# The order list of an adaLN block on one core, solved anew, with two more products of zeros

## The chip, the cores and the metric

The kernel runs on one core of one Trainium2 chip. The metric is device time in microseconds (us) for one execution. Three runs of the kernel before took 416.54, 415.92 and 416.29 us, median 416.29. The engines named below are TensorE (PE; its weight loads are PEld), VectorE (DVE), ScalarE (ACT), GpSimd (POOL) and SyncE (SP), which here only issues DMAs.

## The reference

An adaLN-conditioned block on 2048 tokens of width 576, all in bf16 at the borders:

```
mod = silu(c) @ w_mod                       # six rows of 576: sa, ca, ga, sb, cb, gb
h = layernorm(x) * (1 + ca) + sa
q, k, v = split(h @ wqkv)                   # 32 heads of 18
phi(t) = [softmax(t @ w_phi), softmax(-(t @ w_phi))]     # 36 features a head
kv = phi(k)^T v ; z = sum(phi(k)) ; o = phi(q) kv / (phi(q) z + 1e-6)
x = x + ga * (o @ wo)
h = layernorm(x) * (1 + cb) + sb
x = x + gb * (relu(h @ w1) @ w2)            # hidden width 4608
```

## The kernel before

The tokens stand in 16 tiles of 128. Everything up to the sum `kv` must have seen all tokens; after it, the feed-forward part runs on eight pairs of tiles (`block(n)`, unchanged by the edit), almost without a pause on PE.

To save products, the kernel folds `w_phi` into the key and query weights and the scale `1 + ca` into all three projections. That is the head of the program. For the keys (weights cut into five row chunks of 128, the last of 64):

- `LK.i` loads the key weights: `LK.1` holds chunks 2 and 3, `LK.2` chunk 4, `LK.0` chunks 0 and 1. `WT.c` (`fold_T`, L329) turns chunk c on PE with six transposes into a PSUM tile, and `WTE.c` copies the result out.
- `F1.c` (`fold`, L339) multiplies the turned chunk by the block-diagonal of `w_phi` (built by `WBD` on DVE). Its PSUM tile is copied out in two parts, `FA1.c` (432 columns) and `FB1.c` (144 columns).
- `SIL` computes silu(c); `MC1.0` and `MC1.1` (`first_mods`, L307) make the shift and the scale as columns, each with 25 products of one column. `MSH` and `MSC` copy them out on DVE.
- `B1`, `Bv` and `B0` (`fold_bias`, L360) make the bias rows of keys, values and queries from the shift; `BE...` copy them out. `SC1.c`, `SCv.c`, `SC0.c` scale the chunks of the three weights.
- For x: `LP` and `LP4` load tiles, `LS.t` are the layernorm sums on DVE, `RS.u` the two activations for the factor, `LX.u` the normalisation. `PT.u` (L256) turns the first two pairs on PE, `PX.u.i` copies them out; the later tiles are turned by DMA (`LT.t`, issued by SP).
- `F0`, `FA0`, `FB0` do for the queries what `F1`, `FA1`, `FB1` do for the keys; their turned weights come by DMA (`LQ.c`).

Then come the projections `K.t`, `V.t`, `Q.t` (`project`, L438), each ten products, with copies `KE`, `VE`, `QE`; the softmax steps of the keys (`MN`, `MX`, `LO`, `HI`, `EX`, `SU`, `SA`, `RC`, `SC`) and queries (the same with a q); the rows of the second modulation (`LM`, `RW`, `RWE`, `RC2`, `RD`); the sum `KVa`, `KVb`, `KVc` (L616) with its copies `KVE`; the first pair's attention (`NU` to `WOE`); and the first feed-forward pair (`G`, `FW`, `RL`, `Y`, with the weights `LW` and `W2`).

The order of all this work is written out as a list of names in the string `order`; no scheduler touches SP, PE, DVE and ACT. Each engine runs its own instructions strictly in the list's order. A name's digits are its arguments. For copies and scalings a last argument picks the engine: for most `.1` is ACT and none is DVE; for `KE`, `VE` and `QE` none is ACT and `.1` is DVE. Where a step waits for another engine, everything behind it on its own engine waits too.

PSUM tiles of the products come from `mm_tile`, three buffers in turn: a step that opens a tile waits until the tile opened three steps before has been copied out. The modulations and the products of zeros use `aux_tile`, two buffers in turn.

A product of zeros is the step `Z.k`, whose number has no meaning: one product of 512 columns that nobody reads. One more runs before the list begins.

```
    def fill(n):
        ps = aux_tile("ps_warm")
        for _ in range(n):
            T_.matmul(ps[:], lhsT=zeros[:, 0:P], rhs=zeros[:], start=True, stop=True)
```

The places where the list is run:

```
    for step in order.split():
        name, *at = step.split(".")
        steps[name](*map(int, at))
```

Of the kernel before, what the change touches and what calls it, by code (L numbers as in the profile page):

```python
# [44 lines left out]
def kernel(  # L45
# [23 lines left out]
    V, A_, G, T_ = nc.vector, nc.scalar, nc.gpsimd, nc.tensor  # L69
# [841 lines left out]
    }  # L911

    order = """
    LH LK.1 WT.3 LP.1 WTE.3.1 WT.2 LS.2 WTE.2.1 LK.2 WT.4 WTE.4.1 WBD LK.0 WT.1 LS.3 F1.2 LP.0 WTE.1 F1.3 FB1.2
    LS.1 SIL F1.1 FA1.2.1 RS.1 LX.1 FA1.3.1 LS.0 WT.0 FA1.1.1 FB1.3.1 F1.4 LA.0 FB1.1.1 WTE.0.1 LA.1 Z.2 PT.1
    PX.1.1 FA1.4.1 F1.0 FB1.0 FB1.4 FA1.0.1 MC1.0 LV MSH LP4.2 PX.1.0 RS.0 LX.0 MC1.1 B1 LQ.2 MSC SC1.4 SC1.0
    SC1.2 LQ.3 BE1.0.1 BE1.1.1 SC1.3 LQ.0 PT.0 Bv LP4.4 SCv.0 PX.0.1 SCv.1 SC1.1.1 LS.4 SCv.2 PX.0.0.1 BEv.0.1
    OPEN CR K.2 LS.6 LS.5 BEv.1.1 SCv.3.1 SCv.4.1 K.1 LQ.4 PM.0 KE.2 LQ.1 KE.1 LS.7 V.3 VE.3 RS.2 K.0 LX.2 V.0
    V.1 KE.0 VE.0 RS.3 LQ.5 F0.4 F0.3 LT.4 VE.1 FA0.4.1 LP4.6 F0.2 FB0.4.1 PM.2 LT.5 FB0.3.1 FA0.2.1 V.2 LS.8
    FA0.3.1 LS.10 LS.11 LS.9 FB0.2.1 RS.4 LX.3 VE.2 F0.1 FB0.1 LX.4 FA0.1.1 LS.14 LT.7 RS.5 LT.9 LT.6 K.3 KE.3  # L920
    F0.0 FA0.0.1 K.4 PM.1 KE.4 FB0.0 K.5 SC0.4.1 KE.5 LS.13 LX.5 LT.11 LS.15 V.4 LS.12 RS.6 VE.4 MN.0 SC0.2 K.7
    KE.7 K.9 SC0.1.1 KE.9 LT.10 SC0.0.1 LT.8 MX.0 LO.0 V.9 VE.9 RS.7 K.6 KE.6 SC0.3 B0 BE0.0.1 BE0.1 K.11 Q.2
    LO.1 LX.6 LM.1 LM.0 LM.2 KE.11 Q.3 QE.2 HI.0 Q.1 Q.0 LX.7 EX.0 MX.1 HI.1 MN.1 QE.3 QE.1 QE.0 K.10 KE.10 SU.0
    SA.0 EX.1 LO.2 RW.1 RWE.1.1 RW.0 HI.2 EX.2 LT.13 LT.15 RWE.0 K.8 qMX.0 PM.3 KE.8 qMN.0 SU.1 K.15 KE.15 V.5
    RC.0 VE.5 V.11 VE.11 LO.3 HI.3 LT.12 MX.2 WOL LT.14 V.14 RC2.0 K.12 EX.3 VE.14 SC.0 RC2.2 Q.7 qHI.0 QE.7
    qLO.0 SA.1 SD.6 SD.7 KE.12 RC.1 qEX.0 K.13 KE.13 SU.2 K.14 KE.14 V.12 MN.2 LO.5 LO.4 SA.2 HI.5 VE.12 W1
    LW.0.0 MX.3 LW.2.0 qEX.1 Q.4 RC.3 QE.4 HI.4 MN.3 RC.2 LW.2.1 RC2.1 LW.1.1 RD.2 V.8 VE.8 V.15 qSU.0 V.7 Q.14
    LO.6 EX.5 qSA.0 VE.15 VE.7 EX.4 SC.3 Q.13 SC.1 Q.8 SU.4 SA.4 HI.6 QE.14 SC.2 LW.1.0 QE.13 QE.8 LO.7 HI.7
    qRC.0 SU.5 SA.5 RC.4 Q.10 V.6 QE.10.1 qSC.0 SC.4 EX.6 VE.6 V.10 SU.6 SA.6 EX.7 V.13 SU.7 VE.10 RC.5 RD.0
    VE.13 SC.5 RC.6 SA.7 SC.6 RC.7 SC.7 qT.0 KVa MCE2 KVb KVc WS.0 Q.12 KVE.1 KVE.0.1 NU.1 Q.9 LW.0.1 QE.12 WS.1  # L930
    NU.0 NUE.1 OT.1 OTE.1 QE.9 Q.6 QE.6 NUE.0 OT.0 OTE.0 WO.1 WO.0 WOE.1 S2.1 Q.11 WOE.0 S2.0 QE.11 R2 X2 Q.15
    Q.5 QE.5 P2 W2.0.0 W2.0.1 LW.3.0 QE.15 W2.2.0 PN PNE G.0 W2.1.0 qMX.1 qMN.2 RL.0 qMN.1 FW.2 qLO.1 qHI.1 RL.2
    FW.1 RL.1 RD.1 qEX.3 LW.3.1 W2.1.1 W2.2.1 qEX.2 G.1 RL.3 qSD.3 FW.4 qSD.2 RL.4 qRC.1 qSC.1 FW.5 qMX.2 qHI.2
    qT.1 RL.5 G.2 RL.6 FW.7 FW.8 NV.0 qLO.2 qEX.4 qSD.4 Y.0.0.0 RL.8 Y.0.0.1 qEX.5 RL.7 NVE.0 OU.0 NV.1 Y.1.0.0
    Y.1.0.1 NVE.1 qSD.5 OU.1 WP.0 WPE.0 Y.1.1.0 S3.0 WP.1 WPE.1 S3.1 R3 qRC.2 Y.0.0.2 Y.1.1.1 Y.1.0.2 X3 XT
    YE.0.0 qSC.2 qT.2 Y.0.1.0 MD.0 YE.1.0 Y.0.1.1 MD.4 MD.3 MD.2 MD.1 Y.0.1.2 Y.1.1.2 YE.1.1 YE.0.1
    """
    for step in order.split():
        name, *at = step.split(".")
# [101 lines left out]
```

## Time and profile before

| | us |
|---|---|
| median of three runs | 416.29 (415.92 to 416.54) |
| the profiled execution | 416.63 |
| its span, first to last instruction | 414.5 |
| PE busy in the span | 406.0 (98%) |
| PE, weight loads | 331.2 (80%) |
| DVE busy | 237.4 (57%) |
| ACT busy | 174.2 (42%) |

The busy times are sums over stages of different kinds. A row of a timeline begins with the start and the length of a group in us; then come the engine, the line of the kernel, the operation with its tiles, shapes and count, and in brackets how long the engine had been idle before, and what ended it. A row of the waits gives the total, the times and the longest wait. A row of a table by stretches gives for each engine its busy time and, in brackets, its instructions.

### The profile page before, as it was taken

To read this page: it belongs to the slowest core of one execution; us is meant where nothing else is said; L and a number is where in the kernel's file an instruction comes from. 1 tells how busy PE (TensorE), PEld (TensorE's weight loads), DVE (VectorE), ACT (ScalarE), POOL (GpSimd) and SP (SyncE) were. 2 spreads that over 40 slices of the span, in tenths; PEclk is the share of its full clock that TensorE was granted. 3 is DMA by queue.
4 is the path that set the end of the run, shared out by engine and by line. 5 is a ranking of instruction groups with operands and counts; after the bars stand their busy time and mean duration, and the time that the engine had idled before them with its cause. 6 is when DMAs were issued, how large, how long until landed. Compare 5 with 4: busy or idle time off the path is not lost.

```text
span 414.5 us, 9208 instructions
## 1 busy us (share of the span) xinstructions
PE 406.0 (98%) x3953; PEld 331.2 (80%) x3953; DVE 237.4 (57%) x612; ACT 174.2 (42%) x279; POOL 11.8 (3%) x39
## 2 busy tenths in 40 slices
PE   6999999999999999999999999999999999999997
PEld 5777777787888788788878887888888888878876
DVE  7879999996776665547345552846192533230011
ACT  5687889945671064016302630452055014302400
POOL 8100010000000000000000000000000000000000
PEclk9999999999999999999999999999999999999999
DMA  8956967079931820502051014204210502010001
GB/s 250 251 118 156 237 157 217 1 144 369 321 72 32 118 47 2 115 16 33 15 102 32 17 33 84 47 2 69 61 35 2 117 18 31 16 32 16 0 2 30
DMA packets 72161, 35.43 MB, mean 85 GB/s; under 512 B 56689, under 2 KB 69754, under 8 KB 72122
## 3 DMA queue, kind: packets, MB, share of 16 engines
q1 hardware_dynamic: 71520, 34.83, 35.9%
q8 instruction: 31, 0.51, 0.5%
q10 hardware_dynamic: 602, 0.02, 0.1%
q14 instruction: 8, 0.07, 0.0%
HBM read 19.27 MB, written 2.37 MB: 52 GB/s over the span
## 4 chain that ended last, share of the span: by engine, by line
PE 87%; DVE 7%; DMA 2%; ACT 2%; issue 1%; SPq 1%; DVEq 0%; ACTq 0%
PE ps_y L849 34%; PE ps_h L806 31%; PE ps_h L798 4%; PE ps_v L438 3%; PE ps_wo L714 3%; PE ps_k L438 3%; PE ps_q L438 2%; DMA x_sb<-in_A_x_dram 2%; PE ps_sum L504 2%; PE ps_wo L438 2%; DVE bst L223 2%; DVE phik L528 1%; PE ps_num L657 1%; PE ps_bias L360 1%; DVE xn L232 1%
## 5 line engine op out<-in xcount | busy, mean ns | idle before, releaser
L811 ACT ACTIVATE H<-ps_h 128x1024 bf16<-128x1024 f32 x72 | 73.7, 1023 | 171.1 <-PE ps_h L798 122.5
L849 PE MATMUL ps_y<-w_sb,H 128*128 128x288 bf16 (+2 forms) x1188 | 143.0, 282 | 0.0
L849 PEld LDWEIGHTS <-H 128*128 128x128 bf16 x1188 | 113.7, 98 | 27.3
L806 PE MATMUL ps_h<-hT,w1a 128*128 128x256 bf16 x640 | 74.9, 273 | 0.3 <-DVE hT L408 0.3
L806 PEld LDWEIGHTS <-w1a 128*128 128x128 bf16 x640 | 61.2, 98 | 9.9 <-issue 2.7
L857 DVE TENSOR_TENSOR outt<-ps_y,row_gb 128x288 bf16<-128x288 f32 (+2 forms) x33 | 14.8, 448 | 85.6 <-PE ps_y L849 85.6
L806 PE MATMUL ps_h<-hT,w1b 128*128 128x256 bf16 x512 | 58.9, 273 | 0.0
L438 PEld LDWEIGHTS <-hT 128*128 128x128 bf16 x480 | 46.4, 98 | 13.4 <-issue 1.2
L806 PEld LDWEIGHTS <-w1b 128*128 128x128 bf16 x512 | 49.9, 98 | 6.5 <-issue 0.6
L719 DVE TENSOR_TENSOR x_sb<-x_sb,ps_wo 128x288 bf16<-128x288 bf16 x28 | 12.7, 454 | 32.8 <-PE ps_wo L714 24.8
L223 DVE BATCH_NORM_STATS2 bst<-x_sb 128x6 f32<-128x288 bf16 x64 | 25.8, 444 | 2.1 <-DMA x_sb<-in_A_x_dram 2.0
L232 DVE TENSOR_SCALAR xn<-x_sb,mv,rstd 128x576 bf16<-128x576 bf16 x32 | 12.2, 424 | 22.1 <-ACT rstd L228 22.1
L438 PE MATMUL ps_k<-wfold,hT 128*128 128x270 bf16 (+1 forms) x160 | 22.1, 288 | 0.3 <-ACT pq L89 0.3
L438 PE MATMUL ps_v<-wv_sb,hT 128*128 128x288 bf16 x160 | 21.4, 286 | 0.2 <-ACT room L89 0.2
L438 PE MATMUL ps_q<-wfold,hT 128*128 128x270 bf16 (+1 forms) x160 | 21.1, 285 | 0.0
L515 DVE TENSOR_REDUCE ln_s<-room 128x66 f32<-128x1188 bf16 x14 | 19.1, 1367 | 3.0 <-ACT room L497 3.0
L798 PE MATMUL ps_h<-hT,w1c 64*128 64x256 bf16 x288 | 19.9, 271 | 0.0
L497 ACT ACTIVATE room<-room 128x1188 bf16<-128x1188 bf16 x16 | 18.9, 1187 | 1.9 <-DVE room L468 1.4
L497 ACT ACTIVATE phik<-phik 128x2376 bf16<-128x2376 bf16 x8 | 17.5, 2182 | 0.6 <-DVE phik L470 0.5
L798 PEld LDWEIGHTS <-w1c 64*128 64x128 bf16 x288 | 12.1, 94 | 5.2 <-issue 3.6
L457 DVE TENSOR_TENSOR tree<-tree 128x264 bf16<-128x264 bf16 (+2 forms) x48 | 14.6, 305 | 1.7
L408 DVE TENSOR_SCALAR hT<-hT,mod 128x256 bf16<-128x256 bf16 x35 | 9.7, 342 | 5.0 <-DMA hT<-xn 5.0
(146 smaller groups left out, 347.8 us busy)
## 6 DMA issues: line engine op xcount, KB each, us to landing
w_sb<-in_B_w_dram SPq DMA_DIRECT2D x6, 864.0 KB, 12.4
out_dram<-outt SPq DMA_DIRECT2D x15, 144.0 KB, 1.7
w1b<-in_B_w_dram SPq DMA_DIRECT2D x2, 1024.0 KB, 10.9
x_sb<-in_A_x_dram SPq DMA_DIRECT2D x3, 576.0 KB, 4.3
w1a<-in_B_w_dram SPq DMA_DIRECT2D x2, 768.0 KB
wma<-in_w_mod_dram SPq DMA_DIRECT2D x2, 576.0 KB, 5.8
wmb<-in_w_mod_dram SPq DMA_DIRECT2D x1, 1152.0 KB, 7.3
wmb<-in_w_mod_dram SPq DMA_DIRECT2D x2, 576.0 KB, 8.8
```

What stands on the lines that cost most here:

```text
L223: V.bn_stats(out=st[:, half, :], in_=x_sb[:, t0 + j, half * 288:(half + 1) * 288])
L232: V.tensor_scalar(out=xn[:, j, 0:D], in0=x_sb[:, t0 + j, :], scalar1=mv[:, j, 0:1], scalar2=rs[:, j:j + 1], op0=ALU.subtract, op1=ALU.mult)
L438: T_.matmul(ps[:, 0:cn], lhsT=lhs[:, ci, :], rhs=w[:, ci, cs:cs + cn], start=(ci == 0), stop=(ci == KC - 1))
L457: V.tensor_tensor(out=a[:, :, 0:w], in0=a[:, :, 0:w], in1=a[:, :, w:2 * w], op=op)
L497: A_.activation(out=E[:, j:j + k], in_=E[:, j:j + k], func=ACT.Exp)
L515: V.tensor_reduce(out=t["l", b][:, k * 22:(k + 1) * 22].rearrange("p (g s) h -> p g s h", s=2), op=ALU.add, axis=mybir.AxisListType.X, in_ ...
L719: V.tensor_tensor(out=xs[:, cs:cs + cn], in0=xs[:, cs:cs + cn], in1=p[:, 0:cn], op=ALU.add)
L798: T_.matmul(f1[q][:, e, hh * w:hh * w + w], lhsT=w1["c"][r, 2 * q + hh, :], rhs=hT[r, 4, :], start=(first and hh == 0), stop=(not first an ...
L806: T_.matmul(f1[q][:, e, hh * w:hh * w + w], lhsT=w1_at(2 * q + hh, e, ci), rhs=hT[:, ci, :], start=(first and hh == 0 and ci == 0), stop=( ...
L811: A_.activation(out=p2t["H1"].rearrange("p (e j) n -> p e j n", e=2)[:, :, 2 * q:2 * q + 2], in_=f1[q][:].rearrange("p e (h n) -> p e h n" ...
L849: T_.matmul(ps[:, 0, 0:cn], lhsT=p2t["H1"][:, k, j * P:(j + 1) * P], rhs=p2t["w2"][:, k, c], start=(k == 0), stop=(k == NJ - 1))
L857: V.tensor_tensor(out=o[:, c], in0=ps[:, 0, 0:cn], in1=rows["gb"][:, c], op=ALU.mult)
```

## The change

The string `order` is replaced by another order of the same steps. The list has 450 steps instead of 448: the one `Z` step (between `F1.4` and `PT.1`) becomes three, `Z.1` ahead of all else, `Z.6` between `F1.3` and `F1.1`, `Z.0` between `F1.2` and `WT.0`. Some copies and scalings change engines. To ACT: `PX.1.1`, `FB1.0`, `FB1.4`, `PX.0.1`, `SCv.1`, `SCv.2`, `FB0.0`, `FB0.1`, `SC0.2`, `RWE.0`, `QE.10`. To DVE: `FA1.3`, `BEv.1`, `SCv.4`, `FB0.4`, `VE.5`. The order of PE changes: `WT.1` now stands before `WT.4`, `Bv` before `PT.0`, `K.0` before `K.1`, and much further on. On DVE, `LX.1` and `SIL` now stand before `FB1.2`, and `LS.1` behind `PX.1.0`. On SP, `LP4.6` stands before `LT.4`, and of the six `W2` loads `W2.0.0` and `W2.2.0` are now issued last. The diff, cut to the head and to where the sum `kv` and the `W2` loads stand:

```
-    LH LK.1 WT.3 LP.1 WTE.3.1 WT.2 LS.2 WTE.2.1 LK.2 WT.4 WTE.4.1 WBD LK.0 WT.1 LS.3 F1.2 LP.0 WTE.1 F1.3 FB1.2
-    LS.1 SIL F1.1 FA1.2.1 RS.1 LX.1 FA1.3.1 LS.0 WT.0 FA1.1.1 FB1.3.1 F1.4 LA.0 FB1.1.1 WTE.0.1 LA.1 Z.2 PT.1
-    PX.1.1 FA1.4.1 F1.0 FB1.0 FB1.4 FA1.0.1 MC1.0 LV MSH LP4.2 PX.1.0 RS.0 LX.0 MC1.1 B1 LQ.2 MSC SC1.4 SC1.0
-    SC1.2 LQ.3 BE1.0.1 BE1.1.1 SC1.3 LQ.0 PT.0 Bv LP4.4 SCv.0 PX.0.1 SCv.1 SC1.1.1 LS.4 SCv.2 PX.0.0.1 BEv.0.1
-    OPEN CR K.2 LS.6 LS.5 BEv.1.1 SCv.3.1 SCv.4.1 K.1 LQ.4 PM.0 KE.2 LQ.1 KE.1 LS.7 V.3 VE.3 RS.2 K.0 LX.2 V.0
...
-    VE.13 SC.5 RC.6 SA.7 SC.6 RC.7 SC.7 qT.0 KVa MCE2 KVb KVc WS.0 Q.12 KVE.1 KVE.0.1 NU.1 Q.9 LW.0.1 QE.12 WS.1
...
-    Q.5 QE.5 P2 W2.0.0 W2.0.1 LW.3.0 QE.15 W2.2.0 PN PNE G.0 W2.1.0 qMX.1 qMN.2 RL.0 qMN.1 FW.2 qLO.1 qHI.1 RL.2
-    FW.1 RL.1 RD.1 qEX.3 LW.3.1 W2.1.1 W2.2.1 qEX.2 G.1 RL.3 qSD.3 FW.4 qSD.2 RL.4 qRC.1 qSC.1 FW.5 qMX.2 qHI.2
+    Z.1 LK.1 LP.1 LK.2 WT.3 LK.0 LP.0 LH WT.2 WTE.3.1 WT.1 LS.2 WTE.2.1 WT.4 WTE.4.1 WBD F1.3 LS.3 Z.6 WTE.1
+    F1.1 RS.1 LA.0 F1.2 FA1.3 Z.0 LX.1 FB1.3.1 SIL LA.1 FB1.2 FA1.1.1 FA1.2.1 FB1.1.1 WT.0 WTE.0.1 F1.4 FA1.4.1
+    PT.1 PX.1.1.1 FB1.4.1 F1.0 FB1.0.1 MC1.0 FA1.0.1 LS.0 MC1.1 PX.1.0 LV LS.1 RS.0 MSH CR MSC SC1.1.1 LX.0
+    SCv.4 SCv.2.1 SC1.0 B1 SC1.3 Bv BE1.0.1 BEv.1 BE1.1.1 PT.0 BEv.0.1 PX.0.0.1 PX.0.1.1 SC1.2 SC1.4 OPEN PM.3
+    PM.2 PM.0 LP4.2 LQ.1 PM.1 LS.4 K.2 KE.2 LQ.3 SCv.0 K.0 LS.5 SCv.3.1 LQ.4 LS.7 LS.6 K.1 LP4.4 LS.8 SCv.1.1
+    LS.9 KE.0 RS.2 V.1 KE.1 LQ.2 RS.3 VE.1 LX.2 V.3 LX.3 VE.3 V.0 LQ.0 LQ.5 F0.4 FB0.4 LS.11 LP4.6 RS.4 LX.4
+    LS.10 VE.0 FA0.4.1 F0.3 FA0.3.1 LS.15 LS.13 F0.2 V.2 FB0.3.1 LT.4 FA0.2.1 FB0.2.1 F0.1 VE.2 K.3 LT.5 FB0.1.1
...
+    RC.6 KVa LW.0.1 RC2.2 RD.2 SA.7 QE.10 VE.12 SC.6 RC.7 SC.7 KVb KVc RD.0 WS.1 Q.12 qT.0 KVE.0.1 WS.0 KVE.1
...
+    MCE2 R2 QE.11 Q.15 X2 Q.5 P2 W2.1.0 W2.2.1 W2.0.1 LW.3.0 W2.1.1 QE.15 QE.5 PN RD.1 PNE qMN.1 G.0 RL.0 FW.2
+    qLO.1 RL.2 LW.3.1 FW.1 qMX.1 qHI.1 qMN.2 qEX.2 RL.1 G.1 FW.5 FW.4 qSD.2 qEX.3 qSD.3 qRC.1 RL.3 RL.4 qMX.2
+    qSC.1 RL.5 W2.0.0 G.2 FW.7 RL.6 FW.8 W2.2.0 RL.7 qT.1 NV.0 qLO.2 qHI.2 NVE.0 OU.0 Y.0.0.0 Y.1.0.0 qEX.5 RL.8
```

More of the change, by code (lines that the diff above doesn't have):

```diff
@@ L919 @@
[L919 to L928, printed above, removed]
@@ L929 @@
-    qRC.0 SU.5 SA.5 RC.4 Q.10 V.6 QE.10.1 qSC.0 SC.4 EX.6 VE.6 V.10 SU.6 SA.6 EX.7 V.13 SU.7 VE.10 RC.5 RD.0
-    VE.13 SC.5 RC.6 SA.7 SC.6 RC.7 SC.7 qT.0 KVa MCE2 KVb KVc WS.0 Q.12 KVE.1 KVE.0.1 NU.1 Q.9 LW.0.1 QE.12 WS.1
-    NU.0 NUE.1 OT.1 OTE.1 QE.9 Q.6 QE.6 NUE.0 OT.0 OTE.0 WO.1 WO.0 WOE.1 S2.1 Q.11 WOE.0 S2.0 QE.11 R2 X2 Q.15
-    Q.5 QE.5 P2 W2.0.0 W2.0.1 LW.3.0 QE.15 W2.2.0 PN PNE G.0 W2.1.0 qMX.1 qMN.2 RL.0 qMN.1 FW.2 qLO.1 qHI.1 RL.2
-    FW.1 RL.1 RD.1 qEX.3 LW.3.1 W2.1.1 W2.2.1 qEX.2 G.1 RL.3 qSD.3 FW.4 qSD.2 RL.4 qRC.1 qSC.1 FW.5 qMX.2 qHI.2
@@ L934 @@
-    qT.1 RL.5 G.2 RL.6 FW.7 FW.8 NV.0 qLO.2 qEX.4 qSD.4 Y.0.0.0 RL.8 Y.0.0.1 qEX.5 RL.7 NVE.0 OU.0 NV.1 Y.1.0.0
-    Y.1.0.1 NVE.1 qSD.5 OU.1 WP.0 WPE.0 Y.1.1.0 S3.0 WP.1 WPE.1 S3.1 R3 qRC.2 Y.0.0.2 Y.1.1.1 Y.1.0.2 X3 XT
-    YE.0.0 qSC.2 qT.2 Y.0.1.0 MD.0 YE.1.0 Y.0.1.1 MD.4 MD.3 MD.2 MD.1 Y.0.1.2 Y.1.1.2 YE.1.1 YE.0.1
+    Z.1 LK.1 LP.1 LK.2 WT.3 LK.0 LP.0 LH WT.2 WTE.3.1 WT.1 LS.2 WTE.2.1 WT.4 WTE.4.1 WBD F1.3 LS.3 Z.6 WTE.1
+    F1.1 RS.1 LA.0 F1.2 FA1.3 Z.0 LX.1 FB1.3.1 SIL LA.1 FB1.2 FA1.1.1 FA1.2.1 FB1.1.1 WT.0 WTE.0.1 F1.4 FA1.4.1
@@ new lines @@
+    FA0.1.1 F0.0 KE.3 LT.9 RS.5 FA0.0.1 FB0.0.1 K.4 SC0.3 LT.7 LT.8 LT.6 SC0.0.1 KE.4 K.5 KE.5 V.4 SC0.1.1 VE.4
+    K.9 K.7 KE.9 V.9 MN.0 KE.7 K.6 VE.9 SC0.2.1 KE.6 LS.14 MX.0 LS.12 LO.1 B0 SC0.4.1 BE0.0.1 RS.6 RS.7 HI.1 K.8
+    KE.8 LX.5 BE0.1 Q.2 QE.2 Q.0 LO.0 HI.0 QE.0 MX.1 MN.1 LM.1 EX.0 Q.3 QE.3 LX.7 LO.3 LM.2 LT.11 LM.0 Q.1 K.11
+    LX.6 QE.1 SU.0 RW.1 SA.0 HI.3 RW.0 LO.2 HI.2 KE.11 V.5 LT.10 RWE.1.1 EX.1 RWE.0.1 K.10 KE.10 LT.15 LT.13
+    VE.5.1 K.15 qMX.0 MX.2 qHI.0 EX.3 qMN.0 KE.15 WOL Q.7 Q.4 SU.1 QE.7 SA.1 qLO.0 RC2.0 LT.14 MN.2 EX.2 QE.4
@@ new lines @@
+    RC.0 V.8 VE.8 LO.4 HI.4 K.13 KE.13 LO.5 V.14 V.11 VE.14 HI.5 SD.6 SD.7 LT.12 K.12 W1 VE.11 LW.2.1 EX.4 SC.0
+    Q.8 KE.12 QE.8 V.6 RC.1 K.14 VE.6 KE.14 MN.3 MX.3 V.13 VE.13 RC.3 V.7 VE.7 Q.13 SU.2 Q.14 qEX.0 qEX.1 qSU.0
+    SC.1 LO.6 SA.2 HI.6 EX.5 QE.14 V.10 QE.13 qSA.0 RC.2 SU.5 VE.10 V.15 SU.4 LW.2.0 LW.0.0 SC.3 LW.1.1 RC2.1
+    SA.5 LO.7 HI.7 qRC.0 EX.6 Q.10 SA.4 RC.4 EX.7 SC.2 V.12 qSC.0 SU.6 RC.5 SC.4 SU.7 VE.15 SA.6 LW.1.0 SC.5
+    RC.6 KVa LW.0.1 RC2.2 RD.2 SA.7 QE.10 VE.12 SC.6 RC.7 SC.7 KVb KVc RD.0 WS.1 Q.12 qT.0 KVE.0.1 WS.0 KVE.1
@@ new lines @@
+    NU.1 NUE.1 Q.9 QE.12 NU.0 NUE.0 OT.1 Q.6 OT.0 QE.9 OTE.1 WO.1 OTE.0 WO.0 QE.6 Q.11 WOE.1 S2.1 WOE.0 S2.0
+    MCE2 R2 QE.11 Q.15 X2 Q.5 P2 W2.1.0 W2.2.1 W2.0.1 LW.3.0 W2.1.1 QE.15 QE.5 PN RD.1 PNE qMN.1 G.0 RL.0 FW.2
+    qLO.1 RL.2 LW.3.1 FW.1 qMX.1 qHI.1 qMN.2 qEX.2 RL.1 G.1 FW.5 FW.4 qSD.2 qEX.3 qSD.3 qRC.1 RL.3 RL.4 qMX.2
+    qSC.1 RL.5 W2.0.0 G.2 FW.7 RL.6 FW.8 W2.2.0 RL.7 qT.1 NV.0 qLO.2 qHI.2 NVE.0 OU.0 Y.0.0.0 Y.1.0.0 qEX.5 RL.8
+    NV.1 NVE.1 Y.0.0.1 qSD.5 OU.1 Y.0.0.2 WP.0 WPE.0 S3.0 qEX.4 YE.0.0 qSD.4 Y.1.1.0 WP.1 WPE.1 S3.1 qRC.2 R3
@@ L937 @@
+    Y.0.1.0 X3 XT Y.1.1.1 qSC.2 MD.4 Y.1.1.2 Y.1.0.1 Y.1.0.2 MD.1 MD.0 YE.1.0 Y.0.1.1 Y.0.1.2 MD.3 MD.2 qT.2
+    YE.0.1 YE.1.1
     """
```

## The prediction

> **What bounds the kernel now.** I read the page first (which engine is full), then the list of what TensorE (PE) waited for, then the order of time of the first 25 us on every engine, since the list is changed most there.
>
> ```profile
> span 414.5 us, 9208 instructions
> PE 406.0 (98%) x3953; PEld 331.2 (80%) x3953; DVE 237.4 (57%) x612; ACT 174.2 (42%) x279; POOL 11.8 (3%) x39
> ```
>
> PE is busy 98% of the span. The list holds the same steps, so apart from the clock only three things can move the time: PE's idle time, cold products, and the copies that release PE. These are the waits behind the head, from the list of waits on PE:
>
> ```profile
> PE ps_kv L616 <- DVE phik L528: 0.4, 1, 0.4
> PE ps_k L438 <- ACT pq L89: 0.3, 1, 0.3
> PE ps_num L657 <- ACT KVZ L628: 0.3, 1, 0.3
> PE ps_h L806 <- DVE hT L408: 0.3, 1, 0.3
> PE ps_v L438 <- ACT room L89: 0.2, 1, 0.2
> ```
>
> Together 1.5 us: more than that cannot be won behind the head. The head on PE, in order of time:
>
> ```profile
> 3.90 1.53 PE L329 MATMUL ps_wT<-ident,wk_raw 128*108 128x128 bf16 x12 [1.42 <-DMA wk_raw<-in_A_wqkv_dram]
> 6.10 1.50 PE L329 MATMUL ps_wT<-ident,wk_raw 128*108 128x128 bf16 x12 [0.68 <-DMA wk_raw<-in_A_wqkv_dram]
> 7.39 1.65 PE L339 MATMUL ps_fold<-room,wT 108*128 108x108 bf16 x18
> 9.08 0.80 PE L329 MATMUL ps_wT<-ident,wk_raw 128*108 128x128 bf16 x6
> 10.52 0.64 PE L339 MATMUL ps_fold<-room,wT 108*64 108x108 bf16 x6 [0.64 <-ACT wk_plain L89]
> 11.09 0.61 PE L207 MATMUL ps_warm<-zeros 128*128 128x512 bf16 x1
> 11.49 1.27 PE L256 MATMUL psT_h<-ident,xn 128*128 128x128 bf16 x10
> 12.56 0.69 PE L339 MATMUL ps_fold<-room,wT 108*128 108x108 bf16 x6
> 13.08 1.47 PE L307 MATMUL ps_mod<-siluc,wma 128*128 128x1 bf16 x50
> 14.49 1.36 PE L360 MATMUL ps_bias<-wk_plain,room 128*1 128x288 bf16 x10
> 15.78 1.25 PE L256 MATMUL psT_h<-ident,xn 128*128 128x128 bf16 x10
> 16.95 1.36 PE L360 MATMUL ps_bias<-room 128*1 128x288 bf16 x10
> 18.25 2.97 PE L438 MATMUL ps_k<-wfold,hT 128*128 128x270 bf16 x20
> 21.05 1.39 PE L438 MATMUL ps_v<-wv_sb,hT 128*128 128x288 bf16 x10
> 22.28 1.39 PE L438 MATMUL ps_k<-wfold,hT 128*128 128x270 bf16 x10
> ```
>
> The clock is read from the starts. From 12.56 to 13.08 six products of 576 columns in all take 0.52 us, 0.90 ns a column. From 21.05 to 22.28 ten of 288 take 1.23 us, 0.43 ns a column. So PE begins at half speed. The twenty products at 18.25 take 2.80 us up to 21.05, and warm they would take 2 x 1.23 = 2.46, so 0.34 us was lost to a cold start: the clock rose about 0.7 us into them, at 18.9 to 19.0. The whole head was cold.
>
> **The head, step by step.** These rows of DVE, ACT and SP carry the prices (the last is one of the same kind of copy, later on):
>
> ```profile
> 1.74 0.57 SPq L157 DMA_DIRECT2D wk_raw<-in_A_wqkv_dram  x1
> 2.35 0.58 SPq L155 DMA_DIRECT2D wk_raw<-in_A_wqkv_dram  x1
> 6.99 0.49 ACT L89 ACTIVATE wT<-ps_wT 108x384 bf16<-108x384 bf16 x1 [0.66 <-PE ps_wT L329]
> 7.75 0.50 DVE L91 COPY wT<-ps_wT 108x768 bf16<-108x768 bf16 x1
> 8.17 0.30 DVE L91 CAST wk_plain<-ps_fold 128x144 bf16<-128x144 f32 x1
> 8.50 0.53 ACT L89 ACTIVATE wk_plain<-ps_fold 128x432 bf16<-128x432 f32 x1 [0.92 <-DVE wk_plain L91]
> 8.93 0.29 ACT L227 ACTIVATE rstd<-mv,eps_t 128x2 f32<-128x2 f32 x1
> 9.24 0.20 ACT L228 ACTIVATE rstd<-rstd 128x2 f32<-128x2 f32 x1
> 9.35 0.44 DVE L295 TENSOR_SCALAR sg<-sg 128x5 f32<-128x5 f32 x1
> 10.13 0.77 DVE L232 TENSOR_SCALAR xn<-x_sb,mv,rstd 128x576 bf16<-128x576 bf16 x2
> 10.81 0.82 DVE L223 BATCH_NORM_STATS2 bst<-x_sb 128x6 f32<-128x288 bf16 x2
> 14.07 0.54 DVE L91 COPY hT<-psT_h 128x768 bf16<-128x768 bf16 x1
> 15.50 1.20 DVE L352 TENSOR_SCALAR wfold<-wk_plain,mod 64x576 bf16<-64x576 bf16 x4
> 40.91 0.45 DVE L91 CAST wfold<-ps_bias 1x288 bf16<-1x288 f32 x1
> ```
>
> *Loads.* SP's first loads keep their order. WT.1 now stands before WT.4, and needs the load issued at 2.35, 0.61 us behind the one that WT.4 needs. PE started WT.4 at 6.10; WT.1 followed at 6.74 without a gap. So WT.1 can start between 6.10 and 6.74; I take 6.7 (6.10 + 0.61). Both turns (0.64 each) end at 8.0 instead of 7.4.
>
> *Products of zeros.* One costs 0.40 us cold (11.09 to 11.49). Z.1 lies in the gap before 3.90: nothing. Z.6 and Z.0 put 0.8 us on PE, but what follows waits longer for copies (next step), so nothing on the path; without that wait they would cost their 0.8. The old Z.2 (0.40 between F1.4 and PT.1) goes; the walk below counts from F1.4 on without it.
>
> *The way to F1.4.* F1.3 runs 8.0 to 8.5, drained 8.7. FA1.3 goes to DVE: 432 columns, from the two f32 copies (0.30 for 144, 0.45 for 288) 0.60, so to 9.3. ACT's other half waits for it: the row at 8.50 shows that ACT and DVE read one PSUM tile one after the other. DVE then does LX.1 (9.3 to 10.0, its factors ready at 9.2 behind WTE.4's 0.49 and two of 0.29 and 0.20), the SIL steps (0.78, from 9.35 to 10.13) to 10.7, and only then FB1.2, to 11.0. ACT's FA1.2.1 waits for that: 11.5; FB1.1.1: 11.75. F1.4 needs the tile they free: 11.8, now 10.52. PE is done with WT.0 at 11.1 and waits 0.7.
>
> *From F1.4 to K.2, clock risen by about 12.2 (my choice, argued below).* F1.4 to 12.3, PT.1 to 12.85 (half of the 1.07 from 11.49 to 12.56), drained 13.05. PX.1.1.1 is now ACT's: 0.6, to 13.7; PX.1.0 on DVE behind it: 14.2. LS.1 has been put behind that on DVE: 0.82 and a sum of 0.2, to 15.2; the shift that B1 needs comes behind LS.1: 15.35. PE has F1.0 and the fifty one-column products (1.41, bound by something other than columns, so unchanged) done at 14.5 and waits 0.85. B1 and Bv at half of 1.2 each: 16.6. DVE: crep, scale, LX.0 to 16.5; three scalings of 0.3 to 17.35; BEv.1 0.45, 17.75; SC1.2 and SC1.4, 18.35. K.2 starts at 18.35, warm: 0.10 later, 0.34 faster: **-0.24 us**.
>
> *The same, cold.* PT.1 ends at 13.4, the shift comes at 15.9, B1 and Bv end at 18.4, BEv.1 waits for them until 18.65, and SC1.4 ends at 19.7. K.2 starts there, warm: +1.45 - 0.34 = **+1.1 us**.
>
> **Which clock.** What PE did without rise: 6.10 to 9.7 (transposes and folds, one gap of 0.2), 10.52 to 14.49 (the last 1.4 us one-column products). With rise: 14.49 to about 18.95, 4.46 us of products and transposes with short gaps. Afterwards PE is busy from 6.7 to 11.1 (4.4 us) and again from 11.8 to 12.85. That is as much as preceded the rise, and of real products (folds and zeros) 2.3 us in 8.0 to 10.4 plus 0.5, against 1.2 + 0.7 in the 3.2 us before the rise (16.95 to 18.1 and 18.25 to 18.95). So I take the early rise, at 2 in 3; nothing in the trace fixes the threshold.
>
> [...]
>
> **Behind the head.** K.0 waits for ACT's copies of PT.0, both of them ACT's now: +0.15. After K.2, ACT takes over from DVE PX.0.1, SCv.1, FB0.1, FB0.0, SC0.2, RWE.0 and QE.10, and gives up VE.5 and FB0.4. At the prices of like work above (0.54 for PX.0.1; 0.3 each for FB0.1, FB0.0, SCv.1, SC0.2; 0.45 for RWE.0; 0.6 for QE.10; back 0.6 for VE.5 and 0.3 for FB0.4) that is 1.9 us more on ACT by DVE's prices; I take 2.5, an estimate, as a copy on ACT need not be as short. ACT has this room:
>
> ```profile
> 20.00:50.00 30.00, 29.54 (x285) 22.81 (x287) 26.71 (x75) 25.10 (x64) 0.46 (x1) 1.00 0.80 173
> ```
>
> In 20 to 50 us ACT idles 4.9 us of 30, DVE 3.3, PE 0.46. Following ACT's new order, I find PE waiting about 0.35 at V.2 (FA0.4.1 behind DVE's FB0.4) and 0.1 at Q.2, in place of 0.2 and 0.3: 0. LP4.6 is issued ahead of LT.4 on SP, so DVE no longer waits for it; but DVE then meets VE.5.1 before V.5 is there. I keep the 0.4 at KV (bounds: 0 and 0.8). KVE's two copies change order on the same path: 0. The W2 loads that Y.0.0.0 needs first are now issued last:
>
> ```profile
> w_sb<-in_B_w_dram SPq DMA_DIRECT2D x6, 864.0 KB, 12.4
> 99.60 5.24 SPq L762 DMA_DIRECT2D w_sb<-in_B_w_dram  x2
> 122.22 2.95 PE ps_y L849 x24
> ```
>
> The last of the six is issued by 104.8 and lands by 117.3, 4.9 us before its first use: 0, unless SP is held up by that much. The blocks after the list are unchanged.
>
> **Sum.** The profiled run took 416.63 us (span 414.5 and 2.1 around it), 0.34 above the median of 416.29. 416.63 - 0.24 + 0.15 + 0 = **416.5 us**, own range 415.8 to 417.1.
>
> **Rivals.**
> 1. *The clock does not rise early, or is lost again.* For it: two long busy stretches did not raise it, PE waits 0.7 at 11.1, and 12.85 to 15.35 holds little but one-column products and a wait. Against: the count above. It decides if B1 (15.4 to 16) still starts cold. Then +1.1 and 0.15 on 416.63: 417.9, and 417.4 if 0.5 of the waits behind the head is caught up. Slower. This is also the case that the change does not do what it says.
> 2. *ACT becomes the bound in 20 to 50.* For it: 2.5 us more against 4.9 of room, in an order where PSUM tiles are freed by ACT. Against: PE's copies there wait for PE, mostly. Half of the 2.5 on the path: 417.7.
> 3. *The waits behind the head go too.* For it: DVE has less to do and x_sb arrives earlier. Against: my walk finds others in their place. With 1.3 of the 1.5 us gone: 415.2. Faster.
>
> [...]
>
> **How the numbers follow.** Forecast 0.44, clock 0.30, ACT 0.10, waits gone 0.16. This kernel's measurement tells about 0.2% (0.8 us) from no change: under 415.46 faster, over 417.12 slower. Faster: 0.16 and 0.02 of the forecast; slower: 0.34 of rivals 1 and 2 and 0.02 of the forecast; the rest same, 0.46. The range 415.3 to 418.0 leaves out about 1 in 10 at each end.
>
> **What would show it.** L329's third group six deep starting near 6.7; F1.4 near 11.8 waiting for ACT; L256 at 0.055 us a transpose in PT.1 (right) or 0.107 (rival 1); B1 near 15.35 behind DVE's L315; the first ps_k of L438 near 18.35. Wrong would be: K.2 before 17.5 (then DVE's order costs less than I say), or PE waits over 1 us in 20 to 90.

## The result

The changed kernel took 420.05 us, median of four runs (418.57 to 420.36); the kernel before, beside it, 416.42 (415.92 to 417.06). The ratio is 1.0082, 95% interval 1.0056 to 1.0108: slower by 0.8%, 3.6 us, outside the forecast range of 415.3 to 418.0. The profiled execution took 420.04 us, its span 418.1. The first lines of the changed kernel's page, and its list of what PE waited for up to 125 us:

```profile
span 418.1 us, 9213 instructions
PE 407.2 (97%) x3954; PEld 331.6 (79%) x3955; DVE 236.1 (56%) x605; ACT 176.4 (42%) x286; POOL 11.5 (3%) x39
```

```profile
PE ps_v L438 <- DMA hT<-xn: 2.8, 1, 2.8
PE ps_wT L329 <- DMA wk_raw<-in_A_wqkv_dram: 1.9, 2, 1.1
...
PE ps_fold L339 <- ACT wk_plain L89: 0.7, 1, 0.7
PE ps_bias L360 <- DVE room L316: 0.5, 1, 0.5
...
PE ps_h L806 <- ACT room L89: 0.3, 1, 0.3
...
PE ps_v L438 <- ACT room L89: 0.2, 1, 0.2
```

Behind the head, the waits of before at `ps_kv` (0.4), `ps_k` (0.3) and `ps_num` (0.3) are gone. In their place stands one wait of 2.8 us that was not there. PE in order of time, first the head, then the stretch with that wait:

```profile
6.49 1.52 PE L329 MATMUL ps_wT<-ident,wk_raw 128*108 128x128 bf16 x12 [1.08 <-DMA wk_raw<-in_A_wqkv_dram]
...
11.62 0.64 PE L339 MATMUL ps_fold<-room,wT 108*64 108x108 bf16 x6 [0.66 <-ACT wk_plain L89]
12.18 1.25 PE L256 MATMUL psT_h<-ident,xn 128*128 128x128 bf16 x10
13.22 0.69 PE L339 MATMUL ps_fold<-room,wT 108*128 108x108 bf16 x6
13.75 1.48 PE L307 MATMUL ps_mod<-siluc,wma 128*128 128x1 bf16 x50
15.71 1.36 PE L360 MATMUL ps_bias<-wk_plain,room 128*1 128x288 bf16 x10 [0.48 <-DVE room L316]
16.86 1.41 PE L360 MATMUL ps_bias<-room 128*1 128x288 bf16 x10
18.20 0.81 PE L256 MATMUL psT_h<-ident,xn 128*128 128x128 bf16 x10
18.85 4.10 PE L438 MATMUL ps_k<-wfold,hT 128*128 128x270 bf16 x30
22.80 2.37 PE L438 MATMUL ps_v<-wv_sb,hT 128*128 128x288 bf16 x18
```

```profile
58.87 1.39 PE L438 MATMUL ps_k<-wfold,hT 128*128 128x270 bf16 x10
63.04 4.15 PE L438 MATMUL ps_v<-wv_sb,hT 128*128 128x288 bf16 x20 [2.78 <-DMA hT<-xn]
67.03 1.39 PE L438 MATMUL ps_k<-wfold,hT 128*128 128x270 bf16 x10
68.26 1.39 PE L438 MATMUL ps_q<-wfold,hT 128*128 128x270 bf16 x10
```

The ten transposes from 12.18 take 1.04 us, 0.10 each: cold, as in before. From 63.04 two things go wrong. `V.14` starts 2.78 us after PE ran out of work, and it and `V.11` take 3.99 us up to 67.03, where the next ten products take 1.23. The table by stretches says why these twenty are slow (the number behind the engines, here 0.70, 0.50 and 0.95, is the mean granted clock of the stretch):

```profile
62.00:64.00 2.00, 0.96 (x5) 0.60 (x6) 1.97 (x3) 1.92 (x7) 0.31 (x1) 0.70 0.62 121
64.00:66.00 2.00, 2.00 (x10) 1.29 (x9) 1.97 (x3) 0.34 (x1) 0.00 (x0) 0.50 0.83 175
66.00:68.00 2.00, 2.00 (x18) 1.55 (x16) 2.00 (x3) 1.08 (x3) 0.00 (x0) 0.95 1.10 379
```

Half speed for 0.6 of the first stretch of two us, all of the second and 0.1 of the third: from 62.8 to 66.2, 3.4 us. So the clock fell during the wait. This number was 1.00 also ahead of the first rise (in 12 to 14 us here, where the transposes take 0.10 us each; in before from 15 to 18 us, where ten products of 288 columns take 1.3); there it is the spacing of the products that tells the clock.

Who made `V.14` wait is seen on SP, in order of time, then in what SP waited for, in the write on DVE, and in what ACT waited for:

```profile
51.05 2.13 SPq L187 DMA_DIRECT2D wo_sb<-in_A_wo_dram  x2
59.71 0.60 SPq L384 DMA_DIRECT2D mods_d<-room  x1
60.35 2.54 SPq L247 DMA_TRANSPOSE hT<-xn  x2
```

```profile
SPq L384 <- DVE room L468: 6.4, 1, 6.4
```

```profile
58.80 0.77 DVE L468 TENSOR_TENSOR room<-root,pq 128x1188 bf16<-128x1188 bf16 x1
```

```profile
ACT room L89 <- DMA mods_d<-room: 2.4, 1, 2.4
```

L384 is `RC2.0`, the store of four rows of the second modulation; the two transposes behind it are `LT.14` and `LT.12`. The new list has `RC2.0` behind `qLO.0` and ahead of `LT.14`. SP stands 6.4 us at it, waiting for DVE's write at L468 (`qLO.0`, which ends at 59.57) into the tile `room`, and the turn that `V.14` needs stands behind it. In before, `LT.12` and `LT.14` were ahead of `RC2.0`, and `RC2.0` ahead of `qLO.0`; SP there, in order of time:

```profile
53.05 1.28 SPq L247 DMA_TRANSPOSE hT<-xn  x1
54.45 0.60 SPq L384 DMA_DIRECT2D mods_d<-room  x1
```

Back in the changed kernel, ACT then waits 2.4 us as well: its copy for `QE.4` goes into `room` too, and waits until `RC2.0` has been read out.

### The profile page after: what moved, and what is told of

The parts are those of the page before. It is cut to its first block, busy times and chain, and to the rows that moved or that the text cites. A ratio compares the mean times of both kernels' runs of the same rounds, so it can differ in the third digit from the quotient of the medians.

```text
span 418.1 us, 9213 instructions
## 1 busy us (share of the span) xinstructions
PE 407.2 (97%) x3954; PEld 331.6 (79%) x3955; DVE 236.1 (56%) x605; ACT 176.4 (42%) x286; POOL 11.5 (3%) x39
## 4 chain that ended last, share of the span: by engine, by line
PE 92%; DVE 4%; DMA 2%; ACT 1%; SPq 1%; issue 0%; DVEq 0%; ACTq 0%
PE ps_y L849 34%; PE ps_h L806 30%; PE ps_v L438 5%; PE ps_h L798 4%; PE ps_k L438 4%; PE ps_q L438 3%; PE ps_wo L714 3%; PE ps_sum L504 2%; PE ps_wo L438 1%; PE ps_kv L616 1%; DMA wk_raw<-in_A_wqkv_dram 1%; PE ps_num L657 1%; PE ps_bias L360 1%; DMA hT<-xn 1%; DVE bst L223 1%; PE ps_fold L339 0%
## 5 line engine op out<-in xcount | busy, mean ns | idle before, releaser
L719 DVE TENSOR_TENSOR x_sb<-x_sb,ps_wo 128x288 bf16<-128x288 bf16 x28 | 12.6, 454 | 32.0 <-PE ps_wo L714 24.8
L438 PE MATMUL ps_v<-wv_sb,hT 128*128 128x288 bf16 x160 | 23.1, 299 | 2.9 <-DMA hT<-xn 2.8
L438 PE MATMUL ps_k<-wfold,hT 128*128 128x270 bf16 (+1 forms) x160 | 21.6, 285 | 0.0
L798 PEld LDWEIGHTS <-w1c 64*128 64x128 bf16 x288 | 12.1, 94 | 5.1 <-issue 3.8
L457 DVE TENSOR_TENSOR tree<-tree 128x264 bf16<-128x264 bf16 (+2 forms) x48 | 14.6, 305 | 1.7
L520 ACT ACTIVATE ln_s<-ln_s 128x132 f32<-128x132 f32 x16 | 5.0, 315 | 22.6 <-DVE ln_s L515 22.1
```

The lines of the kernel that those rows point to most:

```text
L438: T_.matmul(ps[:, 0:cn], lhsT=lhs[:, ci, :], rhs=w[:, ci, cs:cs + cn], start=(ci == 0), stop=(ci == KC - 1))
L457: V.tensor_tensor(out=a[:, :, 0:w], in0=a[:, :, 0:w], in1=a[:, :, w:2 * w], op=op)
L719: V.tensor_tensor(out=xs[:, cs:cs + cn], in0=xs[:, cs:cs + cn], in1=p[:, 0:cn], op=ALU.add)
L798: T_.matmul(f1[q][:, e, hh * w:hh * w + w], lhsT=w1["c"][r, 2 * q + hh, :], rhs=hT[r, 4, :], start=(first and hh == 0), stop=(not first an ...
```

## The experiments

Theory: `RC2.0`'s place costs 2.8 us of wait and 1.5 us of half-speed products behind it. Rival A: the shared tile costs, wherever the turns stand. Rival B: the new head with its zeros costs the time. All ratios are to runs of the kernel before that were made beside them.

**The changed kernel once more.**

> The changed kernel once more, for its spread and another profile. [...] 418.5 to 420.5 us, median near 419.9. If the wait at V.14 were an accident of one execution, the profile would not show it and the time would be near 415.5 us.

420.11 us (419.48 to 420.72), ratio 1.0107 (1.0079 to 1.0134). The 2.8 us are there again, to the digit, but the clock stays up. PE and the stretches of that execution:

```profile
60.20 1.39 PE L438 MATMUL ps_k<-wfold,hT 128*128 128x270 bf16 x10
64.37 2.62 PE L438 MATMUL ps_v<-wv_sb,hT 128*128 128x288 bf16 x20 [2.78 <-DMA hT<-xn]
66.83 1.39 PE L438 MATMUL ps_k<-wfold,hT 128*128 128x270 bf16 x10
```

```profile
62.00:64.00 2.00, 0.00 (x0) 0.00 (x0) 1.85 (x5) 1.20 (x4) 0.90 (x3) 1.00 0.42 84
```

Its time is the same only because its head was slower: `V.1` started at 24.12 us where it started at 22.80 above (table in the next section). So the fall of the clock is no sure consequence of the wait.

**The turns first.** On SP only, `RC2.0` behind the two turns:

```
-    ... SA.1 qLO.0 RC2.0 LT.14 MN.2 ... SD.7 LT.12 K.12
+    ... SA.1 qLO.0 LT.14 LT.12 RC2.0 MN.2 ... SD.7 K.12
```

> The changed list, with LT.14 and LT.12 moved ahead of RC2.0 on SP and nothing else. Theory (RC2.0 holds up the turn that V.14 needs, and the clock falls behind that wait): the wait of 2.8 us at V.14 goes, the clock stays up (1.6 us), so about 420.0 - 4.4 = 415.6 us. Rival A (the shared tile is what costs: RC2.0 reads it later still, behind two turns, and ACT's QE.4, which writes it, waits over 2.4 us): V.14's wait for the turn goes, but PE then waits for ACT near 62 to 68 us, 417 to 419 us. Rival B (the loss is in the new head and the products of zeros): 419 to 420 us.

417.88 us, ratio 1.0049 (1.0029 to 1.0068). The wait for the turn is gone; PE waits for ACT instead:

```profile
PE ps_v L438 <- ACT room L89: 2.1, 2, 2.0
```

`V.14` needs the PSUM tile that ACT's `QE.4` empties, and `QE.4` waits 2.4 us for `RC2.0`, as in the changed kernel. The 415.6 us of the theory did not come; rival A's 417 to 419 did: a store that goes out late costs through either queue.

**The store back at its early place.**

```
-    ... MX.2 qHI.0 ... SA.1 qLO.0 RC2.0 LT.14
+    ... MX.2 RC2.0 qHI.0 ... SA.1 qLO.0 LT.14
```

> The changed list, with RC2.0 alone moved back ahead of qHI.0 and qLO.0, so that on SP it no longer waits for them. Theory: no wait of SP for DVE there, LT.14 is issued about 6 us earlier, no wait at V.14, no fall of the clock, ACT's wait of 2.4 us gone too: 415.3 to 415.9 us. Rival A predicts the same here but not in the run with the turns first. Rival B: 419 to 420 us.

> The changed list with RC2.0 moved back ahead of qHI.0, once more, as the base of the other three runs here. 415.1 us.

415.11 and, in a second set of runs, 415.39 us; ratios 0.9988 (0.9969 to 1.0006) and 0.9971 (0.9952 to 0.9991). One name moved takes off 4.7 to 5.0 us (medians against the changed kernel's 420.05 and 420.11, not timed side by side). PE goes from `K.13` to `V.14` without a pause:

```profile
58.12 1.39 PE L438 MATMUL ps_k<-wfold,hT 128*128 128x270 bf16 x10
59.35 2.61 PE L438 MATMUL ps_v<-wv_sb,hT 128*128 128x288 bf16 x20
61.80 1.39 PE L438 MATMUL ps_k<-wfold,hT 128*128 128x270 bf16 x10
```

**A tile of its own.** Every step stays where the changed list has it:

```
-        rows["four", i] = room[:, 12176:12752].bitcast(FP32) if i else ...
+        rows["four", i] = wmp.tile([P, 288], FP32, name="row_mods")[:] if i else ...
```

> The changed list, every step at its place (RC2.0 still behind qLO.0 and ahead of LT.14), but the rows that RC2.0 reads (written by RWE.1) get a tile of their own in place of a stretch of the tile room. If what holds RC2.0 is that qLO.0, on DVE, writes another stretch of the same tile: RC2.0 goes out near 53 to 55 us, no wait at V.14, ACT's QE.4 does not wait for it: 414.9 to 415.7 us, as with RC2.0 moved back. If RC2.0 waits there for something of its own: 419.5 to 420.5 us.

416.10 us, ratio 0.9996 (0.9974 to 1.0018). `RC2.0` goes out at once and the turns right behind it:

```profile
54.85 0.60 SPq L384 DMA_DIRECT2D mods_d<-row_mods  x1
55.50 2.54 SPq L247 DMA_TRANSPOSE hT<-xn  x2
```

So it was not its place by itself, but its place together with the shared tile: with `room`, SP waited for DVE's write into another stretch of it. This execution had the slow head too (`V.1` at 24.26). From there to its end it takes 390.9 us, 2.9 less than the changed kernel's second profile (393.8): the wait alone. The median lies 0.4 above the range that I expected; its interval overlaps with both of the store early.

**Work in the wait.** Twelve products that nobody reads, ahead of `V.14`:

```
-    ... LO.5 V.14 V.11
+    ... LO.5 ZL.6 ZL.6 V.14 V.11
+    def fill_late(n):
+        ps = aux_tile("ps_warm")
+        for _ in range(n):
+            T_.matmul(ps[:], lhsT=ident[:], rhs=wfold[0][:, 0, 0:512], start=True, stop=True)
```

> The changed list, with twelve more products that nobody reads (128 rows, 512 columns, about 0.22 us each warm, 2.6 in all) put on PE just ahead of V.14, so that PE works while it waits for the turn; the turn is as late as in the changed kernel. Theory: the wait is as long, but the clock does not fall, so V.14 and V.11 take 2.5 us in place of 4.15: 418.2 to 418.8 us. If the slow products behind the wait have another cause than the clock, or the fall would come anyway: 420 us. If the added products are themselves in the way (the turn no longer late): over 420 us.

418.15 us (417.07 to 419.29), ratio 1.0052 (1.0031 to 1.0073). The turn is as late as ever, `V.14` and `V.11` run warm:

```profile
60.71 2.75 PE L873 MATMUL ps_warm<-wfold,ident 128*128 128x512 bf16 x12
63.65 2.62 PE L438 MATMUL ps_v<-wv_sb,hT 128*128 128x288 bf16 x20 [0.19 <-DMA hT<-xn]
```

Against the changed kernel's 420.1 that is about 1.9 us, an amount that fits the 1.5 us of slow products in the first profile. The two were not timed side by side. The clock stayed up in the changed kernel's second profile too, without these products, so one profile does not show that they hold it up; it is the lower time that speaks for it.

**Old and new heads with old and new rests.** The new head up to `K.2` with the old rest; the old head with the new rest, `RC2.0` early:

```
 first:   + new list up to K.2      + old list, the steps that are left
 second:  - new list up to K.2      + old list up to K.2,  then the new list, the steps that are left
```

> The changed list up to K.2 (with the three products of zeros), followed by the old list's order of all that is left. It prices the new head by itself, against the kernel before. Theory: the head runs cold as in the changed kernel and K.2 starts 0.6 us later, so +0.5 to +1.1: 416.9 to 417.5 us. Rival B: 419 to 420 us. If the head costs nothing: 416.4 us.

> The old list up to K.2, followed by the changed list's order of the rest with RC2.0 moved back ahead of qHI.0. If head and rest add up (new head +1.4 with the old rest, old head taken off here): 415.1 - 1.4 = 413.7 us. If the new head only looks dear beside the old rest and the two do not add up: 415 us or more.

417.52 us, ratio 1.0032 (1.0016 to 1.0048), and 415.18 us, ratio 0.9965 (0.9948 to 0.9982). So the new rest gains 1.2 us once the store is mended; in its list of waits `ps_kv`, `ps_k` and `ps_num` are missing, as in the changed kernel. The new head costs 1.4 us with the old rest and 0.2 with the new one (415.39 against 415.18, intervals that overlap). The two do not add up as I had expected; why not stays open, beyond what the clock does in the head.

**Without the zeros in the list.**

```
-    Z.1 LK.1 ... LS.3 Z.6 WTE.1 ... FA1.3 Z.0 LX.1
+    LK.1 ... LS.3 WTE.1 ... FA1.3 LX.1
```

(on the list with `RC2.0` early)

> The changed list with RC2.0 moved back ahead of qHI.0 and without the three products of zeros in the list. If they do nothing: 415.1 us. If they cost their 0.8 us on the path: 414.3 us. If they bring the early rise of the clock (about 7.5 to 10.5 us) in most runs and that rise is worth something: 415.4 to 415.9 us, with the clock's first rise later in the profile.

416.42 us, ratio 1.0000 (0.9987 to 1.0012), 1.0 us above the same list with zeros. Without them, F1.4 still starts at 11.60 behind ACT, and the head runs cold:

```profile
11.60 0.64 PE L339 MATMUL ps_fold<-room,wT 108*64 108x108 bf16 x6 [1.49 <-ACT wk_plain L89]
12.17 1.25 PE L256 MATMUL psT_h<-ident,xn 128*128 128x128 bf16 x10
```

With them, in the second set of the list with the store early, the same transposes take 0.057 each:

```profile
11.95 0.73 PE L256 MATMUL psT_h<-ident,xn 128*128 128x128 bf16 x10
12.52 0.43 PE L339 MATMUL ps_fold<-room,wT 108*128 108x108 bf16 x6
12.80 1.39 PE L307 MATMUL ps_mod<-siluc,wma 128*128 128x1 bf16 x50
14.96 0.78 PE L360 MATMUL ps_bias<-wk_plain,room 128*1 128x288 bf16 x10 [0.77 <-DVE room L316]
```

So the zeros cost nothing on the path, and the list with them is about 1 us faster. In these two executions an early rise of the clock goes with them (9.6 us against 18.4); of the list without them there is this one profile, and with them the rise was late in three of eight (next section).

**The shift first.** On DVE, `MSH` ahead of `LS.1` (`RC2.0` early):

```
-    ... PX.1.0 LV LS.1 RS.0 MSH CR
+    ... PX.1.0 LV MSH LS.1 RS.0 CR
```

> The changed list with RC2.0 moved back ahead of qHI.0, and with the copy MSH ahead of the sum LS.1 on DVE, so that B1 no longer waits 0.8 us for it. If the head's loss lies in that wait and in the fall of the clock that follows it: B1 starts near 14.2, no or a shorter half-speed stretch after it, 414.0 to 414.6 us. If LX.0, PT.0 and their copies are then late instead: 415.1 us.

414.53 us (414.25 to 415.45), ratio 0.9957 (0.9942 to 0.9972): 0.9 us below the list that it starts from (415.39) and faster than both kernels. B1 follows the one-column products without a wait, warm:

```profile
13.34 1.39 PE L307 MATMUL ps_mod<-siluc,wma 128*128 128x1 bf16 x50
14.68 0.78 PE L360 MATMUL ps_bias<-wk_plain,room 128*1 128x288 bf16 x10
```

**And the keys first.** Besides, `BE1`, `SC1.2` and `SC1.4` ahead of what only the values need:

```
-    ... SCv.4 SCv.2.1 SC1.0 B1 SC1.3 Bv BE1.0.1 BEv.1 BE1.1.1 PT.0 BEv.0.1 PX.0.0.1 PX.0.1.1 SC1.2 SC1.4 OPEN
+    ... SC1.0 B1 SC1.3 Bv BE1.0.1 BE1.1.1 SC1.2 SC1.4 SCv.2.1 BEv.1 PT.0 BEv.0.1 PX.0.0.1 PX.0.1.1 SCv.4 OPEN
```

> The list with RC2.0 ahead of qHI.0 and MSH ahead of LS.1, and besides with what K.2 needs put first behind B1: on ACT, BE1.0 and BE1.1 ahead of SCv.2; on DVE, SC1.2 and SC1.4 ahead of BEv.1 and SCv.4. K.2 waited 0.7 us for ACT's wfold in the run with the shift first. If that wait is on the path: 413.8 to 414.2 us. If V.1 and V.3 wait for the values' weights instead: 414.5 us or more.

414.84 us, ratio 0.9976 (0.9960 to 0.9992): no gain over the last one. `K.2` starts at 17.14, but the next wait takes its place:

```profile
17.14 1.39 PE L438 MATMUL ps_k<-wfold,hT 128*128 128x270 bf16 x10
19.20 2.77 PE L438 MATMUL ps_k<-wfold,hT 128*128 128x270 bf16 x20 [0.68 <-ACT hT L89]
```

## Why the prediction was wrong

**Where the 3.6 us come from**, by single executions. From the start of `V.1` to the end of the span, the four profiled executions of the new list without the wait (the store early twice, a tile of its own, no zeros) take 390.8 to 390.9 us, the turns first 393.0, the two with the late turn and the clock up (the changed kernel's second profile, work in the wait) 393.8, and the one in which the clock fell behind the wait 395.3. So the late turn costs 3.0 us (PE idles 2.78 of them; `V.14` starts 4.17 us after `K.13`, with the store early 1.23), the fall behind it 1.5, and all other differences between these executions lie ahead of `V.1`. The spans add up: before 414.5; the old head with the mended new rest 413.0 (-1.5); the new head with no early rise, which the execution without zeros shows (`V.1` at 22.78, in the changed kernel's first profile at 22.80), 413.6 (+0.6); the late turn, +3.0; the slow products behind it, +1.5. The sum is 418.1, the measured span. By medians the store costs 4.7 to 5.0, and these two terms give 4.5 of that where the clock falls; the rest is open.

**The step that failed is "Behind the head", which I put at 0.** The runs showed 3.0 us there, and 4.5 where the clock fell. Of SP's queue I named `LP4.6`, `LT.4` and the `W2` loads, and did not price `RC2.0`, which the new list moves past `qHI.0` and `qLO.0` and ahead of two turns. What was queued behind it (the turn for `V.14`) and which tile it reads were both to be had: it is one name in the list, and L384 in before's profile is issued at 54.45, ahead of `qLO.0` (60.10). That it waits for a write to another stretch of that tile, only the runs showed. My own line "PE waits over 1 us in 20 to 90" was the one that came true.

**The waits behind the head.** I found others in the place of the old ones, and kept the 0.4 at KV. In fact they went, and nothing of size came in their place: 1.5 us between the two spans, 1.2 between the medians. The three listed waits that went are 1.0 of it, the other two (0.5) stayed. That is rival 3 (1.3), at 0.16, right in its mechanism and hidden under a larger loss. The 0.15 that I gave `K.0` did not come: no wait at `ps_k` is in the first profile's list.

**ACT as the bound (rival 2).** Not seen. In 20 to 50 us ACT was busy 25.8 us where before has 25.1, 0.7 more and not the 2.5 that I took, and PE idled 0.16 there. In 45 to 75 us ACT's longest wait, 2.4 us, was for the store.

**The walk to F1.4** held: WT.1 at 6.49 (6.7 said), F1.4 at 11.62 behind ACT with 0.66 us of wait (11.8 and 0.7). The zeros cost nothing on the path, as said.

**Which clock.** The early rise, at 2 in 3, came in five of the eight executions profiled with this head. What I did not see is that it is lost again around B1 in four of these five: rival 1 had it in its title ("or is lost again"), but priced only the head that stays cold. Rise and fall, read from the record of the granted clock and the spacing of products, and the start of `V.1`, in executions with the same list up to there, with the time from there to the end of the span:

| execution | first rise | half speed again | V.1 starts | V.1 to the end |
|---|---|---|---|---|
| store early, second set | 9.6 | never | 21.55 | 390.8 |
| store early | 11.2 | 14.6 to 18.1 | 22.05 | 390.8 |
| turns first | 9.2 | 16.0 to 19.4 | 22.17 | 393.0 |
| changed kernel, first profile | 18.4 | (at 62.8) | 22.80 | 395.3 |
| work in the wait | 10.7 | 14.2 to 21.0 | 23.41 | 393.8 |
| changed kernel, second profile | 21.7 | never | 24.12 | 393.8 |
| a tile of its own | near 21.6, by the spacing | never | 24.26 | 390.9 |

The eighth, with the old rest (rise at 10.3, half speed again from 13.7 to 20.5), has another list behind `K.2`.

The fall of the second row, in the table by stretches:

```profile
12.00:14.00 2.00, 2.00 (x67) 2.00 (x65) 0.65 (x2) 2.00 (x6) 0.00 (x0) 1.00 1.07 325
14.00:16.00 2.00, 1.23 (x18) 0.70 (x16) 1.75 (x9) 1.14 (x4) 0.00 (x0) 0.66 1.29 210
16.00:18.00 2.00, 2.00 (x20) 1.07 (x17) 1.42 (x5) 1.93 (x5) 0.00 (x0) 0.50 1.21 119
```

It comes behind the fifty one-column products and the 0.77 us of wait at B1. In the two executions in which B1 did not wait (the shift first, the keys first) the clock rose at 12.1 and 11.4 and did not fall again; in the first row it stayed up in spite of the wait. In the third row the clock rose at 9.2 and fell at 16.0. In the first half of that time, 9.2 to 12.6, PE was busy 1.8 us; in the second, 12.6 to 16.0, 2.6 us, 1.4 of them with the one-column products. So the fall came behind the busier half; whether these products have a part in it, no run shows.

My two walks were both too long, by 0.2 to 0.4 us up to B1 and by 0.3 to 0.7 from there: warm, `K.2` came at 17.67 (18.35 said), cold at 18.85 and 19.23 (19.7 said). So -0.24 was not the likely value of the head, nor was +1.1: in the first profile it was +0.6, and the start of `V.1`, 22.16 with the old head and the new rest, spreads over 2.7 us by when the clock rises and falls.

## What to carry to other kernels

When an order is solved anew, go through each DMA queue name by name: what each transfer now waits for, and which transfer that somebody needs stands behind it. Here a small store that reads part of a shared tile waited for the tile's last writer and held up its next one; a tile of its own, or issuing it before the tile is taken over, took the loss away. A wait on PE can cost more than its length (3.0 us in one execution, 4.5 in another), so price it so, and read more than one execution before a clock's rise is counted on.

## What the runs showed of the chip

With the same wait of 2.78 us the clock fell in one execution and not in another. In the first PE stopped at 60.3 and the clock fell at 62.8, 2.5 us later; in the second PE stopped at 61.6 and went on at 64.4, and the granted clock was 1.00 from 62 to 70 us. So the length of the wait did not decide it, and no run shows what did. Five of the profiled executions had a fall. Three of the falls lasted about 3.4 us (62.8 to 66.2, 16.0 to 19.4, 14.6 to 18.1) and two about 6.8 (14.2 to 21.0, 13.7 to 20.5). Falls are common: in at least nine of the ten timed executions of the changed kernel the mean granted clock is 0.996 or less (the one fall of the first profile gives 0.995), and in at least 14 of the 24 with the store early. Where they lie is known of the profiled executions alone.

In the executions with the head of the changed kernel the first rise lay between 9.2 and 21.7 us. The same list up to 9 us led to a rise at 9.2 us in one execution (the turns first) and to none before 21.7 in another (the changed kernel's second profile). In the first PE was busy without a pause from 6.23 us up to the rise, 3.0 us, 1.3 of them with transposes; in the second from 6.40 to 9.79, 3.4 us, 1.3 of them with transposes, and no rise came. So the count of busy time on which I took the early rise was an estimate that these two executions do not bear out, and what decides the rise they do not show.
